# One ring over all PSUM banks, score slots in threes, and the last slot behind the value products (squared-ReLU attention into a SwiGLU block)

## The chip, the cores and the metric

The kernel runs on one core of one Trainium2 chip. A time is the device time of one execution in microseconds, from start to end; several executions give a median. One execution was also recorded by the hardware profiler. Its span runs from the first to the last recorded instruction, so its own time is a little longer than its span.

## The reference: what is computed

Inputs are q, k and v with 8 batch elements, 12 heads, 448 positions and 64 features per head, and three weight matrices (768 x 1536 twice, 1536 x 768) with a gain vector of 768. Cut to what matters:

```python
scores = np.matmul(q, k.transpose(0, 1, 3, 2)) / np.sqrt(64)
attn   = np.maximum(scores, 0.0) ** 2 / 448
x      = np.matmul(attn, v).transpose(0, 2, 1, 3).reshape(8 * 448, 12 * 64)
xn     = x / np.sqrt(np.mean(x * x, axis=-1, keepdims=True) + 1e-6) * rms_g
g      = xn @ w_gate
out    = (g * sigmoid(g) * (xn @ w_val)) @ w_out          # 3584 x 768, float32
```

There is no softmax, so no sum over keys has to be known before the value products start.

## The kernel before

**Units.** Attention is cut into 24 units `m`: batch element `b = m // 3`, and within it `t = m % 3`, four heads (two pairs). Within a unit the scores are computed transposed, keys on partitions and the 448 queries along the row, in seven *slots*. Slots 0 to 2 are the three chunks of 128 keys for the first pair of heads, slots 3 to 5 those for the second pair, and slot 6 holds the last 64 keys of both pairs.

**A slot.** `scores` (line 317) issues a slot's matmuls (line 334). In slots 0 to 5 there are two, one for each head of the pair, and each uses 64 of the 128 rows of TensorE's array; in slot 6 there are four, and each uses one 64 x 64 quadrant. They write a tile of two PSUM banks (`psS`). ScalarE then takes the relu of both banks into an SBUF tile `r` (line 343), and VectorE squares `r` in place (line 310).

**The value products.** `attend(m)` (line 437) multiplies the seven squared slots of a unit with v, into two accumulators `psAV` of one bank each: twelve matmuls of 128 rows by 64 columns for slots 0 to 5, and then four in 64 x 64 quadrants for slot 6. `evacuate` (lines 462 and 464) reads each accumulator on ScalarE, once scaled into `xT`, and from batch element 2 on once more squared into `sq`; VectorE adds up the squares (line 474).

**The dense block.** When the three units of a batch element are done, `norm` (lines 523, 531, 542, 545) makes the normalised rows `xn`. The dense work then stands in a list, `pieces`: 12 *gate* pieces (six matmuls of 448 columns into `psG`, line 614, then Silu on ScalarE, line 622), alternating with 12 *val* pieces (six matmuls into `psV`, line 628, then on VectorE the product of `psV` and the gate's `sig` into `hT`, line 635). After each second batch element come 14 *output* pieces (twelve matmuls of 384 columns into `psO`, line 657; the copy to SBUF alternates between ScalarE, line 673, and VectorE, line 675). The first batch element's dense work is done in smaller pieces (`part_gates`, line 569).

**The order.** Every engine works through its own instructions in the order in which the program issues them; nothing reorders them. The main loop at line 803 interleaves attention and dense work by hand: `fill(us)` issues pieces from the list until their estimated cost has used up `us`. For one unit of the steady part the loop issues: slots 0 and 1 of unit `m`; `attend(m - 1)`; slots 2 and 3; a fill of 0.36 of the unit's `rate`; slots 4 and 5; a fill of 0.36; slot 6; a fill of 0.28. `rate` is 4.0 for the first units, then 12.0, then 13.4. After the last unit the rest of the list is issued.

**PSUM.** PSUM has eight banks. Four of them are two `psS` tiles of two banks, used in turn. The other four are the `rot` tiles of one bank each, used in turn by everything else: gate, val and output pieces, the accumulators, the norm's sum, transposes. The framework in which the kernel is written adds the waits: an instruction that writes into a tile waits, by a semaphore, until those that used the tile before have finished.

The functions that the change touches, with the line numbers that the profile uses:

Of the kernel before, what the change touches and what calls it, by code (L numbers as in the profile page):

```python
# [15 lines left out]
def kernel(  # L16
# [37 lines left out]
    def cols(h):  # L54
# [11 lines left out]
        tc.tile_pool(name="psum", bufs=2, space=bass.MemoryType.PSUM)  # L66
# [12 lines left out]
    nc.vector.memset(ones_bf[:], 1.0)  # L79

# [114 lines left out]
    def transposes(n):  # L195
# [4 lines left out]
        if n < HP:  # L200
            pass
        elif pr == 0 or pr == 1 and e == 0:
            r0, r1 = (HALF, P) if pr == 0 else (0, P)
            if j == 0 and pr == 1:
                big(pr, None)
            ps = psum.tile([P, NU, r1 - r0], BF16, name="psQ", tag="rot", bufs=4)
            for u in range(NU):
                turn(ps[:, u, :], lambda hh: q_t[pr][:, 2 * j + hh, u, :], r0, r1)
            nc.vector.tensor_copy(out=QT[pr][:, j, :, r0:r1], in_=ps[:])
        if b == 1:  # L210
            if j == 0:
                big(None, b)
            ps = psum.tile([P, XT0], BF16, name="psK", tag="rot", bufs=4)
# [7 lines left out]
            nc.vector.tensor_copy(out=KTt[b][:, j, :XT0], in_=ps[:])  # L221
# [18 lines left out]
    def first_q(h, t, pairs=(0, 1)):  # L240
# [3 lines left out]
        ps = psum.tile([P, n, u1 - u0, HALF], BF16, name="psQ", tag="rot", bufs=4)  # L244
# [9 lines left out]
        nc.vector.tensor_copy(out=QT[0][:, j : j + n, u0:u1, :HALF], in_=ps[:])  # L254

    def first_k(t, pairs=(0, 1)):

        w, n, i0 = (S if t else XT0), len(pairs), pairs[0]
        ps = psum.tile([P, n, w], BF16, name="psK", tag="rot", bufs=4)
# [16 lines left out]
        nc.vector.tensor_copy(out=KTt[0][:, j : j + n, :w], in_=ps[:])  # L276
# [9 lines left out]
    def last_keys(m):  # L286

        b, t = divmod(m, ND)
        ps = psum.tile([P, 2, XK], BF16, name="psX", tag="rot", bufs=4)
        for i in range(2):  # L290
            turn(ps[:, i, :], lambda hh: kx_t[b][:, 4 * t + 2 * i + hh, :], 0, XK)
        nc.vector.tensor_copy(out=KTt[b][:, 2 * t : 2 * t + 2, XT0:S], in_=ps[:])
# [4 lines left out]
    def warm_tile():  # L297
        W["ps"] = psum.tile([P, S], FP32, name="psW", tag="rot", bufs=4)

    def warm(k):  # L300
        for _ in range(k):
            nc.tensor.matmul(  # L302
                out=W["ps"][:], lhsT=ones_bf[:, :P], rhs=ones_bf[:], start=True, stop=True
            )
# [12 lines left out]
    def scores(m, slots, k=0, late=None):  # L317
        b, t = divmod(m, ND)
        qt, kt = QT[b // 2], KTt[b]
        for s in slots:  # L320
            warm(k)
            ps = psum.tile([P, 2, 512], FP32, name="psS", tag="psS")
            if s < 2 * NCH:
                i, c = divmod(s, NCH)
                todo = [(2 * t + i, slice(0, P), slice(c * P, (c + 1) * P))]
            else:
                todo = [
                    (2 * t + i, slice(i * XK, (i + 1) * XK), slice(XT0, S))
                    for i in range(2)
                ]  # L330
            for j, rows, keys in todo:
                for hh in range(2):
                    prt = slice(hh * D, (hh + 1) * D)
                    nc.tensor.matmul(  # L334
                        out=ps[rows, hh, :S].rearrange("k (u x) -> k u x", u=NU),
                        lhsT=kt[prt, j, keys],
                        rhs=qt[prt, j, :, b % 2 * HALF : (b % 2 + 1) * HALF],
                        start=True,
                        stop=True,
                    )  # L340
            r = rpool.tile([P, 1024], BF16, name="r", tag="r")
            r = r[:, : 2 * S].rearrange("p (h x) -> p h x", h=2)
            nc.scalar.activation(out=r, in_=ps[:, :, :S], func=ACT.Relu)  # L343
            square(r, late)
            R[m, s] = r
# [4 lines left out]
    def part_scores(h, t, tiles, k=0, late=None):  # L350
# [4 lines left out]
        for x in tiles:  # L355
            warm(k)
            n = len(PARTS[x])
            ps = psum.tile([P, 2, 512], FP32, name="psS", tag="psS")
# [28 lines left out]
    def part_attend(h, t, late=None):  # L387
        w = (US[h][1] - US[h][0]) * HALF
        acc = [psum.tile([P, w], FP32, name="psAV", tag="rot", bufs=4) for _ in range(2)]
# [24 lines left out]
        accs = [(slice(i, i + 1), acc[i][:]) for i in range(2)]  # L414
        evacuate(0, t, accs, cols(h), late)

    def attend(m):
        b, t = divmod(m, ND)
        acc = [psum.tile([P, S], FP32, name="psAV", tag="rot", bufs=4) for _ in range(2)]
# [24 lines left out]
        evacuate(b, t, [(slice(i, i + 1), acc[i][:]) for i in range(2)], slice(0, S))  # L444
# [68 lines left out]
    def norm(b, parts, ready):  # L513
# [6 lines left out]
        ps = psum.tile([P, S], FP32, name="psSS", tag="rot", bufs=4)  # L520
# [39 lines left out]
    def part_gates(h, fbs):  # L560
# [4 lines left out]
        def both(w_sb, fb, name):  # L565
            ps = psum.tile([P, 2, w], FP32, name=name, tag="rot", bufs=4)
# [13 lines left out]
        def gate(fb, st):  # L580
# [3 lines left out]
            ps = both(wg_sb, fb, "psG")  # L584
            sig = tpool.tile([P, 512], BF16, name="sig", tag="sig")
            st["sig"] = sig[:, : 2 * w].rearrange("p (i x) -> p i x", i=2)
            nc.scalar.activation(out=st["sig"], in_=ps[:], func=ACT.Silu)

        def val(fb, st):
            ps = both(wv_sb, fb, "psV")  # L590
# [14 lines left out]
    def gates(b):  # L605
# [3 lines left out]
        def gate(fb, st):  # L609
            if e == 0:  # L610
                HT[pr, fb] = hpool.tile([P, NU, P], BF16, name="hT", tag="hT")
            ps = psum.tile([P, S], FP32, name="psG", tag="rot", bufs=4)
            for kt in range(KT):
                nc.tensor.matmul(  # L614
                    out=ps[:],
# [6 lines left out]
            nc.scalar.activation(out=sig[:, :S], in_=ps[:], func=ACT.Silu)  # L622
            st["sig"] = sig

        def val(fb, st):
            ps = psum.tile([P, S], FP32, name="psV", tag="rot", bufs=4)
            for kt in range(KT):
                nc.tensor.matmul(  # L628
                    out=ps[:],
# [8 lines left out]
                in1=ps[:].rearrange("p (u x) -> p u x", u=NU),  # L638
# [11 lines left out]
    def outproj(pr):  # L650
        ob = out[2 * pr * S : 2 * (pr + 1) * S, :].rearrange("(x u) m -> x u m", u=NU)

        def half(u, o):
            ost = opool.tile([P, OW], FP32, name="ost", tag="ost")
            ps = psum.tile([P, OW], FP32, name="psO", tag="rot", bufs=4)
            for fk in range(FT):
                nc.tensor.matmul(  # L657
                    out=ps[:],
# [13 lines left out]
            if o == 0:  # L672
                nc.scalar.copy(out=ost[:], in_=ps[:])  # L673
            else:
                nc.vector.tensor_copy(out=ost[:], in_=ps[:])  # L675
# [127 lines left out]
    for m in range(ND, N + 1):  # L803
        rate = 4.0 if m < 2 * ND + 1 else 12.0 if m < 4 * ND else 13.4
        quick = 2 if m in (2 * ND, 2 * ND + 1) else 1
        if m > ND:
# [57 lines left out]
```

## Time and profile before

| | before |
|---|---|
| median of 3 runs | 466.06 us (463.85 to 468.08) |
| the profiled execution's own time | 462.43 us |
| its span, first to last instruction | 460.7 us |
| mean granted TensorE clock | 0.999 |
| TensorE matmuls busy | 447.8 us (97% of the span), 3250 instructions |
| ScalarE busy | 271.0 us (59%) |
| VectorE busy | 259.2 us (56%) |
| GpSimd busy | 67.1 us (15%) |

A row of the timeline gives a start in microseconds from the start of the span, a duration, the engine (PE is TensorE's matmuls, PEld its weight loads, ACT is ScalarE, DVE is VectorE), the source line, the operation, output and inputs with their shapes, and how many equal instructions were merged into the row. In brackets stands how long the engine idled before the row and what released it. The end of a matmul is modelled: successive groups overlap by their pipeline's length, so the distance between two starts is the better measure of a group's cost.

### The profile page before, as it was taken

The numbers are of one execution on the slowest core, as the hardware profiler recorded it, in microseconds if no ns is written. First come the engines' busy times: TensorE is split into PE (matmuls) and PEld (weight loads), VectorE is DVE, ScalarE is ACT, GpSimd is POOL, SyncE is SP. The second block draws the span as 40 slices with busy tenths as digits, with TensorE's granted clock in tenths as the row PEclk, the third lists the DMA queues.
The fourth block names the chain that finished last, engine by engine and source line by source line (L and its number), as shares of the span: only waits on it lengthen the run. The fifth ranks groups of instructions, "written<-read, shape, count | busy, mean of one in ns | idle before, by whom it ended". The sixth has DMA issues, their size and how long they took to land.

```text
span 460.7 us, 8008 instructions
## 1 busy us (share of the span) xinstructions
PE 447.8 (97%) x3250; PEld 234.1 (51%) x3250; DVE 259.2 (56%) x466; ACT 271.0 (59%) x414; POOL 67.1 (15%) x72
## 2 busy tenths in 40 slices
PE   7898899999999999999999999999999999999997
PEld 3466565744455544444445544444445555555564
DVE  3576877966467446955576446845476436423111
ACT  3697779767656678655766568665765645222111
POOL 9534312430220017000400010000000000000000
PEclk9999999999999999999999999999999999999999
DMA  9999999999396659900896547000001210000122
GB/s 100 190 194 193 187 171 141 191 164 139 19 175 157 150 121 148 117 18 2 79 129 116 142 113 68 1 2 0 2 34 70 77 61 0 1 0 2 47 98 96
DMA packets 134181, 42.79 MB, mean 93 GB/s; under 512 B 114560, under 2 KB 134144, under 8 KB 134144
## 3 DMA queue, kind: packets, MB, share of 16 engines
q0 software_dynamic: 97056, 24.38, 63.5%
q1 hardware_dynamic: 36944, 17.80, 16.8%
q8 instruction: 25, 0.41, 0.4%
q10 hardware_dynamic: 144, 0.10, 0.1%
q14 instruction: 12, 0.10, 0.1%
HBM read 48.76 MB, written 11.01 MB: 130 GB/s over the span
## 4 chain that ended last, share of the span: by engine, by line
PE 83%; DVE 5%; DMA 4%; ACT 3%; issue 2%; POOL 1%; SPq 1%; ACTq 0%; POOLq 0%
PE psO L657 24%; PE psV L628 20%; PE psG L614 20%; PE psS L334 7%; PE psAV L437 6%; DMA KT<-kld 3%; DMA kld<-in_k_dram 1%; DVE xn L545 1%; ACT r L343 1%; DVE r L310 1%; PE psV L569 1%; PE psG L569 1%; PE psW L302 1%; PE psSS L523 1%; ACT r L382 1%
## 5 line engine op out<-in xcount | busy, mean ns | idle before, releaser
L310 DVE TENSOR_TENSOR r<-r 128x896 bf16<-128x896 bf16 (+4 forms) x171 | 103.2, 614 | 79.9 <-ACT r L343 76.5
L343 ACT ACTIVATE r<-psS 128x896 bf16<-128x896 f32 x147 | 128.6, 930 | 22.4 <-PE psS L334 22.3
L657 PE MATMUL psO<-wo_sb,hT 128*128 128x384 bf16 x672 | 113.2, 327 | 0.7 <-DVE hT L635 0.7
L614 PE MATMUL psG<-xn,wg_sb 128*128 128x448 bf16 x504 | 109.4, 353 | 0.2 <-DVE xn L545 0.2
L628 PE MATMUL psV<-xn,wv_sb 128*128 128x448 bf16 x504 | 109.3, 353 | 0.1
L622 ACT ACTIVATE sig<-psG 128x448 bf16<-128x448 f32 x84 | 46.1, 553 | 79.1 <-PE psG L614 72.9
L657 PEld LDWEIGHTS <-hT 128*128 128x128 bf16 x672 | 64.1, 98 | 47.3 <-issue 5.1
L635 DVE TENSOR_TENSOR hT<-sig,psV 128x448 bf16<-128x448 bf16 x84 | 51.3, 616 | 53.4 <-PE psV L628 51.1
L628 PEld LDWEIGHTS <-wv_sb 128*128 128x128 bf16 x504 | 47.9, 98 | 48.1 <-issue 4.8
L614 PEld LDWEIGHTS <-wg_sb 128*128 128x128 bf16 x504 | 48.0, 98 | 47.2 <-issue 4.0
L673 ACT COPY ost<-psO 128x384 f32<-128x384 f32 x28 | 13.5, 481 | 60.4 <-PE psO L657 46.9
L334 PE MATMUL psS<-QT,KT 64*128 64x448 bf16 (+1 forms) x336 | 44.5, 360 | 1.4 <-DMA KT<-kld 0.8
L675 DVE COPY ost<-psO 128x384 f32<-128x384 f32 x27 | 15.0, 554 | 29.7 <-PE psO L657 28.9
L545 DVE SCALAR_TENSOR_TENSOR xn<-xT,g_sb,rstd 128x448 bf16<-128x448 bf16 (+2 forms) x54 | 31.3, 626 | 0.2
L121 POOL DMA_DIRECT2D vld<-in_v_dram x9 | 8.9, 986 | 152.3 <-PE psAV L437 151.1
L437 PE MATMUL psAV<-r,vld 128*64 128x448 bf16 x252 | 27.8, 357 | 0.0
L542 DVE RECIPROCAL rstd<-rstd 128x112 f32<-128x112 f32 (+2 forms) x32 | 25.2, 823 | 3.5 <-ACT rstd L531 3.5
L334 PEld LDWEIGHTS <-KT 64*128 64x128 bf16 (+1 forms) x336 | 11.6, 96 | 28.0 <-issue 25.6
L382 ACT ACTIVATE r<-psS 128x768 bf16<-128x768 f32 (+3 forms) x24 | 18.5, 830 | 10.0 <-PE psS L371 10.0
L462 ACT ACTIVATE xT<-psAV 128x448 bf16<-128x448 f32 x36 | 19.8, 551 | 4.5 <-PE psAV L437 4.4
L464 ACT ACTIVATE sq<-psAV 128x448 f32<-128x448 f32 x36 | 20.0, 556 | 0.0
L437 PEld LDWEIGHTS <-vld 128*64 128x64 bf16 x252 | 12.5, 109 | 13.8 <-issue 7.4
(59 smaller groups left out, 287.6 us busy)
## 6 DMA issues: line engine op xcount, KB each, us to landing
out_dram<-ost SPq DMA_DIRECT2D x55, 192.0 KB, 2.0
qld<-in_q_dram POOLq DMA_DIRECT2D x7, 672.0 KB, 18.6
kld<-in_k_dram POOLq DMA_DIRECT2D x7, 576.0 KB, 16.0
vld<-in_v_dram POOLq DMA_DIRECT2D x7, 576.0 KB, 7.3
wo_sb<-in_moe_w_out_dram POOLq DMA_DIRECT2D x3, 768.0 KB, 28.0
vxld<-in_v_dram POOLq DMA_DIRECT2D x16, 96.0 KB, 7.3
wg_sb<-in_moe_w_gate_dram POOLq DMA_DIRECT2D x4, 384.0 KB, 14.5
wv_sb<-in_moe_w_val_dram POOLq DMA_DIRECT2D x4, 384.0 KB, 15.4
```

What stands on the lines that cost most here:

```text
L310: nc.vector.tensor_tensor(out=r, in0=r, in1=r, op=ALU.mult)
L334: nc.tensor.matmul(out=ps[rows, hh, :S].rearrange("k (u x) -> k u x", u=NU), lhsT=kt[prt, j, keys], rhs=qt[prt, j, :, b % 2 * HALF : (b % ...
L343: nc.scalar.activation(out=r, in_=ps[:, :, :S], func=ACT.Relu)
L382: nc.scalar.activation(out=r, in_=ps[:, :, : n * w], func=ACT.Relu)
L437: nc.tensor.matmul(out=acc[i][hh * D : (hh + 1) * D, :], lhsT=w[rows, hh, :], rhs=r[rows, hh, :], start=(c == 0), stop=(c == NCH),)
L542: nc.vector.reciprocal(out=rstd[:, cs], in_=rstd[:, cs])
L545: nc.vector.scalar_tensor_tensor(out=xn[:, kt, sl], in0=xt[:, kt, sl], scalar=g_sb[:, kt : kt + 1], in1=rstd[:, :w], op0=ALU.mult, op1=ALU ...
L614: nc.tensor.matmul(out=ps[:], lhsT=wg_sb[:, kt, fb * P : (fb + 1) * P], rhs=xn[:, kt, :], start=(kt == 0), stop=(kt == KT - 1),)
L622: nc.scalar.activation(out=sig[:, :S], in_=ps[:], func=ACT.Silu)
L628: nc.tensor.matmul(out=ps[:], lhsT=wv_sb[:, kt, fb * P : (fb + 1) * P], rhs=xn[:, kt, :], start=(kt == 0), stop=(kt == KT - 1),)
L635: nc.vector.tensor_tensor(out=HT[pr, fb][:, :, e * HALF : (e + 1) * HALF], in0=st["sig"][:, :S].rearrange("p (u x) -> p u x", u=NU), in1=p ...
L657: nc.tensor.matmul(out=ps[:], lhsT=HT[pr, fk][:, u, :], rhs=wo_sb[:, fk, o * OW : (o + 1) * OW], start=(fk == 0), stop=(fk == FT - 1),)
```

## The change: what it does

The two kinds of PSUM tile give way to four tiles `pb0` to `pb3` of two banks each, allocated once. `bank()` hands out one bank (half of such a tile), and `both_banks()` hands out a whole tile. Up to the fourth unit the old division is kept: tiles `pb0` and `pb1` for score slots, the four halves of `pb2` and `pb3` in turn for the rest. From the fifth unit on (`m = 4`) all eight banks are one ring in the order pb0 first half, pb0 second half, pb1 first half, and so on. Each request takes the next bank; a request for both banks first steps over a single half, so that it starts on a whole tile. The two accumulators of `attend` are now the halves of one tile.

The unit is issued in another order. Slots 0, 1 and 2 come together. Then comes `attend(m - 1)`, and directly behind its last matmuls, which work in quadrants, slot 6 of unit `m`. Before the evacuation of the accumulators is issued, the relu of slot 2 is; the relu and the square of slot 6 come behind that evacuation. Then a fill of 0.36, a fill of 0.18, slots 3, 4 and 5 together, and a fill of 0.46.

```diff
     psum = ctx.enter_context(
-        tc.tile_pool(name="psum", bufs=2, space=bass.MemoryType.PSUM)
+        tc.tile_pool(name="psum", bufs=1, space=bass.MemoryType.PSUM)
     )
...
+    banks = [
+        psum.tile([P, 2, 512], FP32, name=f"pb{i}", tag=f"pb{i}") for i in range(4)
+    ]
+    at = {"ring": None, "slot": 0, "rot": 0}
+
+    def bank(n=512, dtype=FP32):
+        if at["ring"] is None:
+            i = 4 + at["rot"] % 4
+            at["rot"] += 1
+        else:
+            i = at["ring"] % 8
+            at["ring"] += 1
+        ap = banks[i // 2][:, i % 2, :]
+        if dtype is BF16:
+            ap = ap.bitcast(BF16)
+        return ap[:, :n]
+
+    def both_banks():
+        if at["ring"] is None:
+            i = at["slot"] % 2
+            at["slot"] += 1
+        else:
+            at["ring"] += at["ring"] % 2
+            i = at["ring"] // 2 % 4
+            at["ring"] += 2
+        return banks[i]
...
-    def scores(m, slots, k=0, late=None):
+    def products(m, s):
...
-            ps = psum.tile([P, 2, 512], FP32, name="psS", tag="psS")
+        ps = both_banks()
...
+    def relu2(m, s, ps, late=None):
+        r = rpool.tile([P, 1024], BF16, name="r", tag="r")
+        r = r[:, : 2 * S].rearrange("p (h x) -> p h x", h=2)
+        nc.scalar.activation(out=r, in_=ps[:, :, :S], func=ACT.Relu)
+        square(r, late)
+        R[m, s] = r
+
+    def scores(m, slots, late=None):
         for s in slots:
...
+            relu2(m, s, products(m, s), late)
...
-    def attend(m):
+    def attend(m, after=None):
         b, t = divmod(m, ND)
-        acc = [psum.tile([P, S], FP32, name="psAV", tag="rot", bufs=4) for _ in range(2)]
+        pair = both_banks()
+        acc = [pair[:, i, :S] for i in range(2)]
...
-        evacuate(b, t, [(slice(i, i + 1), acc[i][:]) for i in range(2)], slice(0, S))
+        if after is not None:
+            after()
+        evacuate(b, t, [(slice(i, i + 1), acc[i]) for i in range(2)], slice(0, S))
...
         def gate(fb, st):
...
-            ps = psum.tile([P, S], FP32, name="psG", tag="rot", bufs=4)
+            ps = bank(S)
...
         def val(fb, st):
-            ps = psum.tile([P, S], FP32, name="psV", tag="rot", bufs=4)
+            ps = bank(S)
...
         def half(u, o):
             ost = opool.tile([P, OW], FP32, name="ost", tag="ost")
-            ps = psum.tile([P, OW], FP32, name="psO", tag="rot", bufs=4)
+            ps = bank(OW)
...
     for m in range(ND, N + 1):
...
+        if m == ND:
...
+            at["ring"] = 2 * (at["slot"] % 2)
+            continue
+        if m % ND == 0:
+            turn_by_dma(len(turns))
+        if m < N:
+            scores(m, (0, 1))
+            third = products(m, 2)
             if m == 2 * ND + 1:
                 fill(0.36 * rate, quick)
+
+            def rest(m=m, third=third):
+                relu2(m, 2, third)
+                last = products(m, 2 * NCH)
+                late.append(lambda: relu2(m, 2 * NCH, last))
+
+            attend(m - 1, rest)
+            flush(late)
+        else:
             attend(m - 1)
-            if m < N:
-                scores(m, (2, 3))
-            fill(0.36 * rate, quick)
+        fill(0.36 * rate, quick)
         if m < N - 1:
             transposes(2 * m + 2)
...
-        if m > ND and m % ND == 0:
+        if m % ND == 0:
             b = m // ND - 1
             norm(b, slice(0, S), lambda b=b: gates(b))
+        fill(0.18 * rate, quick)
         if m < N:
-            scores(m, (4, 5))
-        fill(0.36 * rate, quick)
-        if m < N:
-            scores(m, (6,))
+            scores(m, (3, 4, 5))
         if m + 1 < N:
             transposes(2 * m + 3)
-        fill(0.28 * rate, quick)
+        fill(0.46 * rate, quick)
```

Every other request for a `rot` tile (transposes, the norm's sum, the partial scores and accumulators of the first batch element) becomes a `bank()` or `both_banks()` in the same way. No arithmetic is added or removed.

## Prediction

> **What bounds it now.** I read the page's busy times first, then the chain that ended last, then the timeline of the stages.
>
> ```profile
> PE 447.8 (97%) x3250; PEld 234.1 (51%) x3250; DVE 259.2 (56%) x466; ACT 271.0 (59%) x414; POOL 67.1 (15%) x72
> ...
> PE 83%; DVE 5%; DMA 4%; ACT 3%; issue 2%; POOL 1%; SPq 1%; ACTq 0%; POOLq 0%
> ```
>
> TensorE is busy 97% of the span and makes 83% of the chain. In the list of waits none of its matmuls waits longer than 1.4 us. So whatever makes TensorE wait now lengthens the kernel, and a saving on TensorE shortens it. ScalarE and VectorE have 40% of their time free, but only as long as TensorE runs ahead of them.
>
> The stretch without attention shows how:
>
> ```profile
> 427.56 1.30 PE L614 MATMUL psG<-xn,wg_sb 128*128 128x448 bf16 x6
> ...
> 428.69 1.30 PE L628 MATMUL psV<-xn,wv_sb 128*128 128x448 bf16 x6
> 428.89 0.54 ACT L622 ACTIVATE sig<-psG 128x448 bf16<-128x448 f32 x1 [1.73 <-PE psG L614]
> ...
> 430.10 0.62 DVE L635 TENSOR_TENSOR hT<-sig,psV 128x448 bf16<-128x448 bf16 x1 [1.65 <-PE psV L628]
> ```
>
> A gate begins at 427.56 and the val piece 1.135 us later (piece to piece in this stretch), while Silu still has to read the gate's bank: it runs 428.89 to 429.43. The next piece never waits for the reader of the one before.
>
> **The saving: fewer changes of array shape.** Whenever TensorE goes from dense pieces (128 x 128) to slots (64 x 128), value products (128 x 64) or quadrants (64 x 64), time is lost. Take slot 6:
>
> ```profile
> 197.98 1.30 PE L614 MATMUL psG<-xn,wg_sb 128*128 128x448 bf16 x6
> ...
> 199.20 0.38 PE L334 MATMUL psS<-QT,KT 64*64 64x448 bf16 x4
> ...
> 199.52 1.31 PE L628 MATMUL psV<-xn,wv_sb 128*128 128x448 bf16 x6
> ```
>
> Without it the val piece would start at 197.98 + 1.135 = 199.115; it starts at 199.52. Four quadrants side by side need one pass of 448 columns (1.135/6 = 0.19), so two changes cost 0.405 - 0.19 = 0.215. Slots 4 and 5 at 194.07 give 0.21 in the same way, and the stretch from 203.03 to 205.57 (five changes) 0.58: about 0.11 a change. A unit has nine changes before and six after, over 20 units 60 x 0.11 = **-6.8 us**.
>
> **The cost: halves of one tile wait for each other.** The diff doesn't show this; the order of the built program with its semaphores does. Before, no matmul waits for a reader of another bank. After, the unit of waiting is the two-bank tile: a group that writes the second half waits for the reader of the first half, which is the group issued just before it. The val piece in pb3's second half waits for the Silu that reads pb3's first half. Following each wait value to the instruction that raises its counter, I count 114 such groups from the ring's start on (50 of them gates behind vals, 23 vals behind gates or the norm), and 12 earlier. Behind the waiting matmul all of TensorE stands still.
>
> *A bare wait.* Gate then val: from the rows above, Silu ends 1.87 us after the gate's start, against 1.135: with the restart, 0.80 late. Val then gate: the product ends at 430.72, 2.03 after the val's start: 0.95 late. Output pieces start 1.95 apart; a copy starts 2.15 after its piece (429.83 and 431.98) and takes 0.48 on ScalarE, 0.55 on VectorE: 0.74 and 0.82. The restart takes 0.06, by the one place where an output piece waited for `hT`, which ended at 235.34:
>
> ```profile
> 234.72 0.62 DVE L635 TENSOR_TENSOR hT<-sig,psV 128x448 bf16<-128x448 bf16 x1 [0.70 <-ACT sig L622]
> ...
> 235.40 0.34 PE L657 MATMUL psO<-wo_sb,hT 128*128 128x384 bf16 x1 [0.74 <-DVE hT L635]
> ```
>
> *The first wait behind a value product* is longer, because the reader stands at the end of ScalarE's queue: relu of slots 0, 1, 2, four evacuations, relu of slot 6, and only then a Silu; on VectorE the square of slot 6 stands ahead of the product.
>
> ```profile
> 188.95 0.56 ACT L462 ACTIVATE xT<-psAV 128x448 bf16<-128x448 f32 x1
> ...
> 189.38 0.58 ACT L464 ACTIVATE sq<-psAV 128x448 f32<-128x448 f32 x1
> ...
> 189.80 0.59 ACT L462 ACTIVATE xT<-psAV 128x448 bf16<-128x448 f32 x1
> ...
> 190.22 0.60 ACT L464 ACTIVATE sq<-psAV 128x448 f32<-128x448 f32 x1
> ...
> 203.03 0.55 PE L334 MATMUL psS<-QT,KT 64*128 64x448 bf16 x4
> 203.44 1.73 ACT L343 ACTIVATE r<-psS 128x896 bf16<-128x896 f32 x2 [0.89 <-PE psS L334]
> ...
> 204.77 0.38 PE L437 MATMUL psAV<-r,vxld 64*64 64x448 bf16 x4
> ...
> 205.08 0.55 PE L334 MATMUL psS<-QT,KT 64*128 64x448 bf16 x4
> ```
>
> Evacuations start 0.425 apart, relus 0.81 (two take 1.73), and the first relu starts 0.41 after slot 0. With slot 0 at time 0: relus at 0.41, 1.22, 2.03; evacuations at 2.85, 3.27, 3.70, 4.12; relu of slot 6 at 4.55, over at 5.47; Silu over at 5.90; square from 5.51, product over at 6.66. TensorE needs 0.67 for three slots, 1.26 for the twelve products, 0.19 for their quadrants, 0.32 for slot 6 with its change, 1.24 for the first piece: it is ready at 3.68. So val-gate waits 3.0 (3.2 where a Silu stands before slot 0), gate-val 2.3, and output pieces, ready at 4.5, wait 2.2 (VectorE copy) or 1.4. Units 7 to 23: eight val-gates, 25.2; three gate-vals, one of them 1.6, 6.2; six output pieces 12.4: **43.8 us**.
>
> *The first wait behind slots 3 to 5*, by the same steps: relus over at 2.95, square and product at 4.14; TensorE ready at 2.0: val-gate 2.2 (2.4 behind a Silu), gate-val 1.45, output pieces 1.35 and 0.74. Of 18: seven val-gates or transposes 16.4, five gate-vals 7.25, six outputs 5.05: **28.7 us**.
>
> *The other 70* from unit 7 on are bare: 43 for `hT` (40.9), 13 for Silu (10.4), 9 output pairs (7.3), 5 around the norm, where ScalarE loads its table (1.28) and takes the square root (0.63) first, 2.2 each (11), and 1.8 for tables loaded back: **71.4 us**. A third of these lie behind the last unit.
>
> *Units 4 to 6:* nine waits, priced alike, with transposes among them whose copy queues behind three squares (2.9 each): **17.9 us**. *The 12 earlier:* no row prices all of them; TensorE waited 0.40 for a `QT` copy once before, and some lie beside waits for loads, so between 0 and 10 us; I take **7 us**.
>
> What hides nothing here: DMA queues keep their order and data; loads and output stores have slack (output stores land in 2.0 us), and the value products' own waits (squares, v) are older than before.
>
> Sum: 43.8 + 28.7 + 71.4 + 17.9 + 7 - 6.8 = **+162 us**, on the profiled execution's 462.4: 624. The median shown, 466.06, is 3.6 above that execution; I forecast **626 us**.
>
> [...] In the rows above, the val piece writes its bank (428.69 on) while Silu reads the gate's (428.89 on), undisturbed. [...] The granted clock is 0.999 throughout. [...]
>
> **Rivals.** *Bare waits only:* if ScalarE and VectorE have caught up more than my walk says, all 126 waits cost their bare 0.90 on average (58.6 us over the 65 above that aren't around the norm): 113 - 6.8 = +106, 569 us. For it: the engines gain idle time as TensorE waits. Against: their queue order is fixed. 0.10.
>
> *The clock drops:* my longest gaps are near 3 us, one a unit. At the start, the ten warm-up matmuls of 448 columns (line 302) take 3.85 us, 0.385 each, against 0.19 warm: a cold stretch that loses 1.9 us. If each of 17 gaps brings one, +33: 659 us. Against: the clock stayed up over the small gaps of the first 40 us (TensorE is busy 79% and 94% of the first two stretches of 20 us). 0.10.
>
> *The waits don't bind, on the other side:* if the ring serves as eight independent banks, each wait points eight groups back, and only the shape changes count: 462.4 - 6.8 = 456 us, **faster**. It decides by whether the reader is the group directly before (0.80 or more late) or older than 1.1 us. The wait values say the former. 0.03; 0.01 for no change.
>
> **Range and chances.** My forecast has 0.76. Its unknowns are the long waits (72 us, perhaps a third off either way), units 4 to 6 and the start (25, half off). The range 565 to 670 takes in the bare case and the clock. Chances: faster by over 1%, 0.03; within 1%, 0.01; slower by over 1%, 0.96. About 1% is what a measurement of this kernel can tell from no change.
>
> **What would show it.** In the changed profile: TensorE busy falls to about 75%; its waits are led by the val's product on VectorE (some 50), the Silu and the output copies; behind the last unit, gate and val pieces alternate at 1.135 and 2.09 us; one gap of about 3 us follows each value product; ScalarE's and VectorE's busy times stay at 271 and 259 us. It would be wrong if those gaps are absent, if gaps are far longer than 3 us, or if matmuls of 448 columns take over 0.19 us in the middle.

## The result: 678 us, slower by 46%

| | before | changed |
|---|---|---|
| median of 4 runs each | 465.25 us (463.85 to 468.08) | 678.40 us (676.32 to 681.55) |
| the profiled execution's own time | 462.43 us | 681.55 us |
| its span | 460.7 us | 679.8 us |
| mean granted TensorE clock | 0.999 | 0.907 |

The ratio is 1.4645 (95% interval 1.458 to 1.471). The prediction was 626 us with a range of 565 to 670: the direction and most of the amount were right, and the time lies above the range. Some executions run some per cent slower at a lower granted clock (the kernel before took 481.75 us at 0.982 in one, 462.28 at 0.996 in another); the ratios leave them out, the medians and ranges do not.

The page of the changed kernel, its busy times, the granted clock in 40 slices, and the three costliest groups of matmuls (busy time, mean ns of one, idle time of TensorE ahead of them and what ended most of it):

```profile
PE 507.2 (75%) x3250; PEld 253.1 (37%) x3250; DVE 266.3 (39%) x466; ACT 271.3 (40%) x414; POOL 67.1 (10%) x72
...
PEclk7788788899989987688988988969887999999999
...
L653 PE MATMUL pb<-xn,wg_sb 128*128 128x448 bf16 x504 | 122.6, 384 | 70.0 <-DVE hT L674 63.9
L667 PE MATMUL pb<-xn,wv_sb 128*128 128x448 bf16 x504 | 123.8, 387 | 31.2 <-ACT sig L661 26.4
...
L696 PE MATMUL pb<-wo_sb,hT 128*128 128x384 bf16 x672 | 119.9, 334 | 28.5 <-DVE ost L714 16.6
```

Two things are to be seen. TensorE, which idled 12.9 us before (460.7 - 447.8), now idles 172.6 us (679.8 - 507.2): +159.7. And the same 3250 matmuls are busy 507.2 us instead of 447.8: +59.4. A gate or val matmul took 353 ns on average before and 384 or 387 now, and the granted clock, 0.999 before, is below 0.9 in 21 of the first 30 slices.

The list of waits of the changed kernel (engine, line, what released it: us in total, times, longest) leads with the three that the prediction named:

```profile
PE pb L653 <- DVE hT L674: 63.9, 50, 3.1
PE pb L667 <- ACT sig L661: 26.4, 23, 2.8
PE pb L696 <- DVE ost L714: 16.6, 13, 2.2
```

The timeline of one unit shows both effects in a row:

```profile
163.38 1.31 PE L667 MATMUL pb<-xn,wv_sb 128*128 128x448 bf16 x6
...
165.54 1.00 ACT L375 ACTIVATE r<-pb 128x896 bf16<-128x896 f32 x1
...
166.58 0.62 DVE L340 TENSOR_TENSOR r<-r 128x896 bf16<-128x896 bf16 x1 [0.18 <-ACT r L375]
167.12 0.61 DVE L674 TENSOR_TENSOR hT<-sig,pb 128x448 bf16<-128x448 bf16 x1
167.79 1.85 PE L653 MATMUL pb<-xn,wg_sb 128*128 128x448 bf16 x6 [3.11 <-DVE hT L674]
...
169.44 2.45 PE L667 MATMUL pb<-xn,wv_sb 128*128 128x448 bf16 x6
...
172.67 1.29 PE L653 MATMUL pb<-xn,wg_sb 128*128 128x448 bf16 x6 [0.78 <-DVE hT L674]
```

The val piece at 163.38 is the first one behind a value product. The gate at 167.79 writes the other half of the same tile, so it waits for the val's reader, the product at 167.12, which stands behind the relu and square of slot 6: TensorE idles 3.11 us. Then the second effect: the gate's matmuls slow down, with a granted clock of 0.50 from 168.4 to 171.7, and the val at 169.44 takes 2.45 us for six matmuls, nearly twice the 1.31 of the val at 163.38. The next gate at 172.67 is at full pace again and shows a bare wait of 0.78.

Where the time came from, stretch by stretch. The boundaries are the starts of value products; "busy" and "idle" are TensorE's. "Filled" is a later experiment in which the waits are there but the clock is full from unit 7 on; its column is its stretch less that of before.

| stretch | before | changed | difference | busy | idle | predicted | filled |
|---|---|---|---|---|---|---|---|
| start to `attend(3)` | 55.54 | 78.89 | +23.4 | +11.5 | +11.9 | +7 | +21.1 |
| `attend(3)` to `attend(6)` | 33.79 | 55.86 | +22.1 | +4.5 | +17.6 | +16.9 | +23.5 |
| `attend(6)` to `attend(23)` | 286.52 | 432.32 | +145.8 | +38.6 | +107.2 | +114.3 | +114.3 |
| from `attend(23)` on | 84.85 | 112.73 | +27.9 | +4.8 | +23.1 | +23.8 | +27.9 |
| sum | 460.7 | 679.8 | +219.1 | +59.4 | +159.7 | +162 | +186.8 |

(Predicted, from the prediction's terms: 7; 17.9 less 3 units of 0.34; 43.8 + 28.7 + two thirds of 71.4, less 17 units of 0.34; a third of 71.4.) The row that carries the miss is the third, 31.5 us over the forecast, and then the first.

### The profile page after: what moved, and what is told of

Read it like the earlier page. It is cut to its first block, busy times and chain, and to the rows that moved or that the text cites. A ratio compares the mean times of both kernels' runs of the same rounds, so it can differ in the third digit from the quotient of the medians.

```text
span 679.8 us, 8029 instructions
## 1 busy us (share of the span) xinstructions
PE 507.2 (75%) x3250; PEld 253.1 (37%) x3250; DVE 266.3 (39%) x466; ACT 271.3 (40%) x414; POOL 67.1 (10%) x72
## 3 DMA queue, kind: packets, MB, share of 16 engines
q1 hardware_dynamic: 36944, 17.80, 10.8%
## 5 line engine op out<-in xcount | busy, mean ns | idle before, releaser
L653 PE MATMUL pb<-xn,wg_sb 128*128 128x448 bf16 x504 | 122.6, 384 | 70.0 <-DVE hT L674 63.9
L667 PE MATMUL pb<-xn,wv_sb 128*128 128x448 bf16 x504 | 123.8, 387 | 31.2 <-ACT sig L661 26.4
L375 ACT ACTIVATE r<-pb 128x896 bf16<-128x896 f32 x147 | 127.6, 932 | 39.9 <-PE pb L363 39.0
L696 PE MATMUL pb<-wo_sb,hT 128*128 128x384 bf16 x672 | 119.9, 334 | 28.5 <-DVE ost L714 16.6
L661 ACT ACTIVATE sig<-pb 128x448 bf16<-128x448 f32 x84 | 46.0, 547 | 211.4 <-PE pb L653 208.6
L674 DVE TENSOR_TENSOR hT<-sig,pb 128x448 bf16<-128x448 bf16 x84 | 52.1, 620 | 190.0 <-PE pb L667 190.0
L363 PE MATMUL pb<-QT,KT 64*128 64x448 bf16 (+1 forms) x336 | 40.9, 364 | 0.2 <-DVE KT L250 0.2
L474 PE MATMUL pb<-r,vld 128*64 128x448 bf16 x252 | 27.8, 355 | 0.5 <-DVE hT L631 0.2
L418 ACT ACTIVATE r<-pb 128x768 bf16<-128x768 f32 (+3 forms) x24 | 18.5, 826 | 17.6 <-PE pb L407 17.6
L608 PE MATMUL pb<-xn,wv_sb 128*128 128x192 bf16 (+1 forms) x144 | 17.9, 281 | 8.8 <-DVE QT L238 5.8
L501 ACT ACTIVATE xT<-pb 128x448 bf16<-128x448 f32 x36 | 21.0, 585 | 3.3 <-PE pb L474 3.3
L503 ACT ACTIVATE sq<-pb 128x448 f32<-128x448 f32 x36 | 21.5, 597 | 0.0
## 6 DMA issues: line engine op xcount, KB each, us to landing
wo_sb<-in_moe_w_out_dram POOLq DMA_DIRECT2D x3, 768.0 KB, 23.1
```

The source lines that it names most:

```text
L363: nc.tensor.matmul(out=ps[rows, hh, :S].rearrange("k (u x) -> k u x", u=NU), lhsT=kt[prt, j, keys], rhs=qt[prt, j, :, b % 2 * HALF : (b % ...
L474: nc.tensor.matmul(out=acc[i][hh * D : (hh + 1) * D, :], lhsT=w[rows, hh, :], rhs=r[rows, hh, :], start=(c == 0), stop=(c == NCH),)
L608: nc.tensor.matmul(out=ps[:, i, :], lhsT=w_sb[:, kt, (fb + i) * P : (fb + i + 1) * P], rhs=XN[0][:, kt, sl], start=(kt == 0), stop=(kt == ...
L653: nc.tensor.matmul(out=ps, lhsT=wg_sb[:, kt, fb * P : (fb + 1) * P], rhs=xn[:, kt, :], start=(kt == 0), stop=(kt == KT - 1),)
L661: nc.scalar.activation(out=sig[:, :S], in_=ps, func=ACT.Silu)
L667: nc.tensor.matmul(out=ps, lhsT=wv_sb[:, kt, fb * P : (fb + 1) * P], rhs=xn[:, kt, :], start=(kt == 0), stop=(kt == KT - 1),)
```

## The experiments

My theory after the result: the waits between halves of one tile cost what the prediction says, and the rest, about 50 us, is TensorE's clock, which falls after gaps of 2 to 3 us. Rivals: the new order or the ring by itself costs much of the time; the clock does not matter by itself.

### One request, one tile

```diff
         else:
             i = at["ring"] % 8
-            at["ring"] += 1
+            at["ring"] += 2
```

From the ring's start each request for a bank takes the first half of a whole tile, so no group shares a tile with the one before. Up to the fourth unit all is as in the changed kernel. In unit 7 the bank of slot 2 is written over by the value products before its relu; that slot takes other values there, the work is the same.

> The changed kernel, but from the fifth unit on each request takes a whole two-bank tile in turn (a single request uses its first half), so no group waits for the reader of the group just before it. The first four units keep their halves. Theory 1 (halves wait for each other, and the gaps bring the clock down): the first value products still come some 23 us late, and from there on the saved shape changes are all that is left: 465 + 23 - 7 = 481 us, between 470 and 492, granted clock near 1 behind the first 90 us. Rival (the new order of slots itself holds TensorE up behind ScalarE's queue): the two-bank waits explain only some 100 us, so 560 us or more, with gaps of about 3 us behind every value product still there.

Measured: 487.39 us (486.53 to 492.32), ratio 1.050 (1.042 to 1.059). `attend(3)` is 18.6 us late, `attend(6)` 22.8, `attend(23)` 24.1. So from the ring's start on next to nothing is left of the change's cost, and what is left was there before the ring: the start, where requests still take the halves of `pb2` and `pb3` in turn. In the 74.10 us up to `attend(3)` TensorE's busy time is 6.4 us above that of before and its idle time 12.2.

### Eight tiles of one bank

```diff
-        psum.tile([P, 2, 512], FP32, name=f"pb{i}", tag=f"pb{i}") for i in range(4)
+        psum.tile([P, 512], FP32, name=f"pb{i}", tag=f"pb{i}") for i in range(8)
...
-        ap = banks[i // 2][:, i % 2, :]
+        ap = banks[i][:]
...
-        return banks[i]
+        return banks[2 * i : 2 * i + 2]
...
-        nc.scalar.activation(out=r, in_=ps[:, :, :S], func=ACT.Relu)
+        for hh in range(2):
+            nc.scalar.activation(out=r[:, hh], in_=ps[hh][:, :S], func=ACT.Relu)
```

Ring and order are the change's own, at the start too, but the unit of waiting is the bank. A slot's relu becomes two instructions.

> The changed kernel with eight tiles of one bank in place of four of two, in the same ring and the same order; the relu of a slot becomes two instructions, one for each bank. Theory 1: no half waits for another, so the time is that of before less the shape changes, 465 - 7 = 458 us, between 452 and 464, clock 0.99 or more. Rival (order at fault): 560 us or more. If the doubled relus tell on ScalarE, 465 to 475 us.

Measured: 469.18 us (465.66 to 478.73), ratio 1.010 (1.007 to 1.014), clock 1.0. With the same banks in the same order all but 1% of the slowdown is gone, so the tile as unit of waiting makes it, not the ring. The time is above the 452 to 464 that I expected and in the band given for the doubled relus, but they are hardly what lengthens it: "One request, one tile" has single relus and loses the same 4.2 us in units 4 to 6, and about as much in the units with a norm. The start now costs 2.5 us instead of 23.4. The gain that I had put at 0.34 us a unit is there in most plain units (0.2 to 0.6 from `attend(6)` on), but it is given back: +4.2 in units 4 to 6, and +0.2 to +1.0 in four of the units with a norm (12, 15, 18, 21). The timeline of unit 12 shows how:

```profile
181.11 1.30 PE L671 MATMUL pb<-xn,wv_sb 128*128 128x448 bf16 x6
...
181.73 1.28 ACT L574 ACT_TABLE_LOAD   x1
182.25 1.30 PE L657 MATMUL pb<-xn,wg_sb 128*128 128x448 bf16 x6
...
183.68 1.28 ACT L665 ACT_TABLE_LOAD   x1
...
184.98 0.55 ACT L665 ACTIVATE sig<-pb 128x448 bf16<-128x448 f32 x1
...
185.57 1.30 PE L671 MATMUL pb<-xn,wv_sb 128*128 128x448 bf16 x6 [1.35 <-ACT sig L665]
```

The norm loads one table on ScalarE and the next Silu loads the other back, 2.56 us together; the Silu ends at 185.53. The val piece behind three score slots takes the bank again that this Silu reads, the ring having stepped over one bank, and waits 1.35.

### The long gaps filled

```diff
             i = at["ring"] % 8
             at["ring"] += 1
+            if i % 2 and at["gap"]:
+                spare = banks[(i // 2 + 1) % 4]
+                k, at["gap"] = at["gap"], 0
+                for _ in range(k if n == S else k // 2):
+                    nc.tensor.matmul(out=spare[:, 0, :S], lhsT=ones_bf[:, :P],
+                                     rhs=ones_bf[:], start=True, stop=True)
...
             attend(m - 1, rest)
             flush(late)
+            at["gap"] = 13 if m > 2 * ND else 0
...
             scores(m, (3, 4, 5))
+            at["gap"] = 6 if m > 2 * ND else 0
```

The changed kernel, and from unit 7 on matmuls that compute nothing stand in the gap behind the value products (13) and behind slots 3 to 5 (6).

> The changed kernel with dummy matmuls of 448 columns (13, or 6 before an output piece) in the first gap behind each value product, and 6 (3) in the first gap behind slots 3 to 5, from unit 7 on; they write a bank that is free, and every wait stays. Theory 1 with the clock: the gaps stay as long but are filled, the granted clock behind the first 135 us rises from about 0.92 to 0.97 or more, and the time falls by 20 to 35 us, to 645 to 660 us. Rival (the clock costs nothing, all of the loss is in the waits): 678 us or up to 15 us more, as the dummies that end late delay the next piece.

Measured: 656.19 us (653.49, 658.88), ratio 1.411 (1.396 to 1.426); clock 0.958 (0.99 from 135 us on, where the changed kernel has 0.93). The same place as above, in this kernel's timeline:

```profile
162.74 1.31 PE L678 MATMUL pb<-xn,wv_sb 128*128 128x448 bf16 x6
163.88 2.62 PE L99 MATMUL pb<-ones_bf 128*128 128x448 bf16 x13
167.15 1.29 PE L664 MATMUL pb<-xn,wg_sb 128*128 128x448 bf16 x6 [0.65 <-DVE hT L685]
168.28 1.30 PE L678 MATMUL pb<-xn,wv_sb 128*128 128x448 bf16 x6
```

From the first val piece to the gate it is 4.41 us, as in the changed kernel (163.38 to 167.79): the wait is not shortened. But the gate is followed by the next val after 1.13 us instead of 1.65, and that val is at full pace. Doing useless work on TensorE made the kernel 22 us shorter. That is the clock, and it is about what the theory says for units 7 on.

### Only the halves

```diff
-            ps = psum.tile([P, S], FP32, name="psG", tag="rot", bufs=4)
+            ps = bank(S)
...
-        acc = [psum.tile([P, S], FP32, name="psAV", tag="rot", bufs=4) for _ in range(2)]
+        pair = both_banks()
+        acc = [pair[:, i, :S] for i in range(2)]
```

and so for every request for a `rot` tile, while `at["ring"]` stays `None`: the kernel before with its own order, two tiles for score slots, and its four rotating banks made halves of two tiles. One more thing differs, which the expectation leaves out: `attend` gets its two accumulators from `both_banks()`, so they take one of the two tiles of the score slots instead of two rotating banks.

> The kernel of before in its old unit order and with its old division of PSUM into two score tiles and four rotating banks; only that the four rotating banks are now the halves of two persistent two-bank tiles. Theory 1: 101 groups behind the fourth unit and 12 earlier wait for the reader of the group just before them, 90 us bare, some 35 more behind value products and slots, 30 to 40 for the clock: 610 to 660 us. Rival (the halves cost little, the loss is the ring's or the order's): 465 to 500 us.

Measured: 650.25 us (648.44, 652.06), ratio 1.398 (1.384 to 1.412); clock 0.960. A kernel in the order of before, with nothing added, takes 40% longer. Its waits are led by

```profile
PE pb L667 <- ACT sig L661: 40.1, 58, 2.5
PE pb L363 <- ACT sq L503: 28.2, 17, 1.7
PE pb L474 <- ACT r L375: 17.4, 19, 1.0
PE pb L653 <- DVE hT L674: 15.0, 12, 2.7
```

The second and third row, 45.6 us, come from the accumulators: score slots wait for the evacuation of a tile that is now theirs too, and value products for a slot's relu. The other two are waits between halves, mostly for the Silu, since gates happen to take first halves. TensorE idles 161.1 us (646.7 - 485.6), 148.2 more than before; less the 45.6, about 103 are left for the halves and all else. So this run shows that halves cost much without the new order, but its 1.40 is not their price alone, and that it falls into the expected range of 610 to 660 is partly luck.

### Only the order

The loop of the changed kernel on the tiles of before (`psS` twice, `rot` four times); nothing shares a tile.

```diff
-            at["ring"] = 2 * (at["slot"] % 2)
...
-        ps = both_banks()
+        ps = psum.tile([P, 2, 512], FP32, name="psS", tag="psS")
...
-        pair = both_banks()
-        acc = [pair[:, i, :S] for i in range(2)]
+        acc = [psum.tile([P, S], FP32, name="psAV", tag="rot", bufs=4) for _ in range(2)]
```

> The new unit order alone: PSUM divided as before (two score tiles, four rotating banks, each a tile of its own). Slot 2 now needs the tile of slot 0, and slot 5 that of slot 3, so TensorE waits for a relu (0.41 + 0.92 behind the slot's start, against 0.48 that two slots take: some 0.85 us) twice a unit, 20 units: 34 us; less 7 for the shape changes: 490 us, between 478 and 505, granted clock 0.99. If the order itself were what costs 200 us in the changed kernel: over 560 us.

Measured: 511.30 us (510.63, 511.97), ratio 1.101 (1.093 to 1.108): 21 us more than I expected. Its list of waits is led by one line:

```profile
PE psS L333 <- ACT r L345: 40.7, 41, 2.3
```

Three slots in a row need three tiles, and there are two: the third slot waits about 1 us for the relu of the first, twice a unit. From `attend(7)` on a plain unit costs 1.7 us more than before. So the order by itself is a loss; it needs the ring's extra tiles, which is the part of the change that works. About 10 us more came in units 5 and 6, where TensorE waited 3.1 us for a load of k and the granted clock was 0.85 (the twelve matmuls of a value product behind that wait took 2.45 us, elsewhere 1.32); I take no conclusion from those.

### The order late, on four whole tiles

As before through unit 7; from unit 8 on the change's order, with all eight banks as four tiles of two banks, one per request. In the first version the norm stands one piece earlier.

```diff
+    ring["pool"] = ctx.enter_context(
+        tc.tile_pool(name="ring", bufs=4, space=bass.MemoryType.PSUM)
+    )
+    for m in range(2 * ND + 2, N + 1):
...
+            attend(m - 1, rest)
+            flush(late)
+        fill(0.27 * rate)
...
+            norm(b, slice(0, S), lambda b=b: gates(b))
+        fill(0.27 * rate)
+        if m < N:
+            scores(m, (3, 4, 5))
...
+        fill(0.46 * rate)
```

> A version meant to keep what the change gains: everything as before through unit 7; from unit 8 on the new order on a ring of four two-bank tiles, each request a tile of its own, relu in one instruction; and the norm's sum one piece earlier, so that its table loads end before slots 3 to 5. With eight separate banks the plain units ran 0.2 to 0.5 us faster than before, the units with a norm 0.2 to 1.0 slower, units 4 to 6 together 4.2 slower, the start 2.5 slower. Theory 1: 12 plain units at -0.35 and 4 with a norm at about 0: 465 - 4 = 461 us, ratio to before 0.985 to 0.995. Rival: the change of pools or the norm's units cost as much as is gained: ratio 0.998 to 1.005.

Measured: 463.02 us (460.78 to 468.73, 12 runs), ratio 0.997 (0.992 to 1.001). In the profile the distance from `attend(7)` to `attend(23)` is 2.5 us shorter than before, plain units 0.1 to 0.56 each, the norm units (9, 12, 15, 18, 21) +0.31, +0.07, -0.52, +0.67, -0.19. The second version has the norm where the change puts it (fills of 0.36 and 0.18):

> As the version that keeps everything through unit 7 as before, but with the norm's sum where the change puts it, a piece later. Theory 1: the four units with a norm lose about 1 us each again (the Silu before slots 3 to 5 waits for two table loads of 1.28 and a square root), so 3 to 4 us slower than with the sum a piece earlier. Rival: where the sum stands doesn't matter, within 1 us.

Measured: 469.38 us (463.30 to 478.88, 13 runs) against 467.71 of the same comparison, ratio 1.004 (0.999 to 1.008). Neither interval excludes no change, the two overlap, and the runs of that comparison spread widely. The profiles tell the versions apart: from `attend(7)` to `attend(23)` the second takes 3.5 us longer than the first, within the 3 to 4 expected, and in units 12, 15 and 21, where the val piece now waits for the Silu, 1.1 to 1.3 us each. The gain of the new order without the added waits is thus at most 0.8%, under the 5.4 us (1.2%) that 16 units of 0.34 would give, and I can't tell it from nothing in the times.

### All gaps filled

```diff
+            if i % 2 and at["last"] == i - 1:
+                spare = banks[(i // 2 + 1) % 4]
+                k, at["gap"] = at["gap"] or 4, 0
+                for _ in range(k if n == S else max(3, k // 2)):
+                    nc.tensor.matmul(...)
+            at["last"] = i
```

> The changed kernel with matmuls of 448 columns that compute nothing, into a bank of the next tile, in every gap between the two halves of a tile from the ring's start on: 13 (6 up to unit 6) behind value products, 6 behind slots 3 to 5, 4 elsewhere, half as many before output pieces. The waits stay, since the second half's group still waits for the reader of the first. Theory (waits, and on top of them a clock that falls in the long gaps): mean granted clock 0.97 or more, the matmuls of 448 columns in the middle back to 0.35 mean or less, time 628 to 650. Rival (the clock costs nothing by itself, the filler of the first such run only let ScalarE and VectorE catch up): no lower than that run's 656, and the fillers of the short gaps add to it.

Measured: 648.78 us (648.32, 649.24), ratio 1.395 (1.374 to 1.416); clock 0.966, just under what I expected, because the fillers begin with the ring and the start has a lowered clock here too (0.80, in the changed kernel 0.76). Windows between the same value products as in the table, of the changed kernel (stretch, its length, busy time and number of matmuls, granted clock; the last two columns, of DMA, are not used):

```profile
0.00:78.89 78.89, 59.46 (x613) 0.76 1.46 176
78.89:134.75 55.86, 37.49 (x372) 0.91 1.57 97
134.75:567.07 432.32, 324.02 (x1810) 0.91 0.37 48
567.07:679.80 112.73, 86.24 (x462) 1.00 0.07 25
```

and of this kernel:

```profile
0.00:76.66 76.66, 57.65 (x612) 0.80 1.53 168
76.66:133.99 57.33, 45.95 (x402) 0.87 1.57 113
133.99:534.76 400.77, 368.47 (x2225) 1.00 0.41 52
534.76:647.50 112.74, 107.47 (x575) 1.00 0.07 25
```

The third row is the measurement I wanted. With every wait in place and the clock at 1.00, units 7 to 23 take 400.77 us, 114.3 above before; with the clock at 0.91 they take 432.32. So the waits of these units cost about 114 and the clock about 31.5. In 40 of the 74 filled gaps of this row the next piece starts less than 0.06 us behind the fillers, so some of these may have ended after the wait: 114 is rather an upper bound. In the last row, where only short gaps stand, that is so in 22 of 30, the clock is 1.00 in both kernels, and the fillers change nothing.

### One gap of a chosen length

The kernel before, and in each unit from 8 to 23 one gap made by hand. By one theory gaps of 2 to 3 us are enough for the clock to fall, by the other only longer ones are.

```diff
+    def idle(k):
+        warm_tile()
+        warm(1)
+        for _ in range(k):
+            nc.scalar.copy(out=W["ps"][:], in_=W["ps"][:])
+        warm(1)
...
-        fill(0.28 * rate, quick)
+        if 2 * ND + 1 < m < N:
+            fill(0.14 * rate, quick)
+            idle(1)
+            fill(0.14 * rate, quick)
```

> The kernel before with one gap made by hand in each unit from 8 to 23 (16 of them): one matmul of 448 columns into a spare bank, one ScalarE copy of that bank onto itself, one matmul more. TensorE stands still for the copy and what ScalarE has queued ahead of it, 0.9 to 1.5 us. Both theories: 16 gaps and 32 matmuls of 0.19, +20 to +30 us on the kernel before, and the clock stays at 0.99 or more.

> The same with four copies: gaps of 2.3 to 3.0 us. Theory (the clock falls after gaps of 2 to 3 us): 10 or more of the 16 gaps are followed by a stretch at a lower clock that loses some 2.5 us, mean granted clock 0.93 to 0.97, and the time is 25 to 40 us above what the gaps and the matmuls themselves take (+45 to +55), so +70 to +95 on the kernel before. [...]

> The same with six copies: gaps of 3.3 to 4.0 us. Both theories: nearly all 16 gaps bring a stretch at a lower clock, clock 0.92 to 0.96, +62 to +72 for gaps and matmuls and 35 to 45 for the clock, so +97 to +117 on the kernel before.

Measured: 483.68 us (482.49, 484.87) with one copy, 531.40 (525.37, 537.43) with four, 563.97 (556.50, 571.44) with six, against 464.64. In the profiled executions of the last two the stretch from `attend(3)` to `attend(6)`, ahead of the first gap, is also 17 us longer than before, with waits for loads of k and q (4.3 and 4.8 us with four copies) and a lowered clock behind them (there 0.66 from 70 to 100 us), so I compare from `attend(7)` to `attend(23)`. The other execution of each, 60.7 and 91.9 us above before, agrees with the stretches below.

| copies | gap, mean (range) | gaps followed by a slow stretch | `attend(7)` to `attend(23)`, over before |
|---|---|---|---|
| 1 | 0.75 (0.60 to 0.88) | 0 of 16 | +20.4 |
| 4 | 2.4 (2.25 to 2.52) | 7 of 16 | +57.8 |
| 6 | 3.5 (3.35 to 3.62) | 14 of 16 | +89.9 |

(A slow stretch: a microsecond with a granted clock under 0.8 within the next five.) With four copies the nine units without a slow stretch cost 2.94 us each on average, that is the gap, the two matmuls and the changes around them; 16 of those are 47.0, and the other 10.8 us make 1.5 for each of the seven slow stretches. With six copies 16 x (3.49 + 0.54) = 64.5, which leaves 25.4, 1.8 for each of 14. So gaps of 2.25 to 2.52 us do not leave the clock alone; but I had expected 10 or more of 16, and 2.5 us each, so four copies stay under the +70 to +95 expected, and one copy, with +19.0, just under its +20 to +30. Two of the gaps of the kernel with four copies, of equal length and with the same work behind them:

```profile
198.45 0.35 PE L302 MATMUL psW<-ones_bf 128*128 128x448 bf16 x1 [2.52 <-ACT psW L310]
198.64 1.69 PE L635 MATMUL psV<-xn,wv_sb 128*128 128x448 bf16 x6
200.12 2.45 PE L621 MATMUL psG<-xn,wg_sb 128*128 128x448 bf16 x6
...
220.61 0.35 PE L302 MATMUL psW<-ones_bf 128*128 128x448 bf16 x1 [2.52 <-ACT psW L310]
220.80 1.30 PE L635 MATMUL psV<-xn,wv_sb 128*128 128x448 bf16 x6
221.93 1.30 PE L621 MATMUL psG<-xn,wg_sb 128*128 128x448 bf16 x6
```

Behind the first, the val piece slows down midway and the gate piece runs at half pace throughout; behind the second nothing happens. Here are the microseconds from the one on in which each gap ends (the first busy time is TensorE's, the third number from the end is the granted clock):

```profile
198.00:199.00 1.00, 0.55 (x3) 0.29 (x3) 0.00 (x0) 0.40 (x1) 0.00 (x0) 1.00 0.65 123
199.00:200.00 1.00, 1.00 (x5) 0.48 (x4) 0.00 (x0) 0.00 (x0) 0.00 (x0) 0.70 0.63 121
200.00:201.00 1.00, 1.00 (x4) 0.43 (x3) 0.56 (x1) 0.00 (x0) 0.00 (x0) 0.50 0.35 61
201.00:202.00 1.00, 1.00 (x5) 0.32 (x3) 0.06 (x1) 0.00 (x0) 0.00 (x0) 0.50 0.00 0
202.00:203.00 1.00, 1.00 (x6) 0.13 (x4) 0.00 (x0) 0.39 (x1) 0.00 (x0) 0.59 0.00 0
203.00:204.00 1.00, 1.00 (x13) 0.58 (x12) 0.01 (x1) 1.00 (x3) 0.00 (x0) 1.00 0.00 0
...
220.00:221.00 1.00, 0.39 (x3) 0.20 (x3) 0.88 (x2) 0.53 (x2) 0.00 (x0) 1.00 4.30 142
221.00:222.00 1.00, 1.00 (x7) 0.54 (x6) 0.00 (x0) 0.00 (x0) 0.00 (x0) 1.00 4.07 148
222.00:223.00 1.00, 1.00 (x7) 0.42 (x5) 0.80 (x2) 0.00 (x0) 0.00 (x0) 1.00 4.57 144
223.00:224.00 1.00, 1.00 (x10) 0.37 (x10) 1.00 (x2) 0.73 (x2) 0.00 (x0) 1.00 4.66 144
224.00:225.00 1.00, 1.00 (x16) 0.44 (x10) 0.36 (x2) 1.00 (x2) 0.00 (x0) 1.00 4.74 160
225.00:226.00 1.00, 1.00 (x10) 0.35 (x11) 0.81 (x2) 1.00 (x3) 0.00 (x0) 1.00 2.88 90
```

So the length of a gap gives only a chance, here 7 of 16; I leave open what else decides.

## Why the prediction was wrong where it was

**TensorE as the bound, and the halves as the cost: right.** Taking the sharing away (one request, one tile; eight tiles) takes the slowdown away from the ring's start on. Putting the sharing into the order of before brings most of the idle time back, though not all of that run's 1.40 is its doing. TensorE's busy share is 75%, as forecast, the named waits lead, and ScalarE's busy time stays at 271.3; VectorE's rose from 259.2 to 266.3, which I did not follow up (the product that the gates wait for takes 620 ns on average, 616 before).

**Sizes of the waits: right.** Behind the last unit gate and val pieces start 1.13 and 2.08 us apart in turn, where 1.135 and 2.09 were forecast:

```profile
621.34 1.29 PE L653 MATMUL pb<-xn,wg_sb 128*128 128x448 bf16 x6 [0.78 <-DVE hT L674]
...
622.47 1.30 PE L667 MATMUL pb<-xn,wv_sb 128*128 128x448 bf16 x6
...
624.55 1.29 PE L653 MATMUL pb<-xn,wg_sb 128*128 128x448 bf16 x6 [0.78 <-DVE hT L674]
```

The first wait behind a value product was priced 3.0 and is 3.11 where shown. Over units 7 to 23 the terms come to 114.3, and the kernel with all gaps filled measures 114.3; so close a sum owes something to errors that cancel. One pair is known: of the saving of 5.8 us in this sum the kernel with eight tiles shows 0.6, so the waits themselves took at most some 115 where 120 were priced. Behind the last unit 23.8 were priced and 27.9 measured.

**The clock: the step that failed.** The prediction's sum has no term for a lowered clock. That the clock would stay up behind gaps of 3 us was my assumption, which no run shows: no matmul of before waited longer than 1.4 us. The rival *The clock drops* got 0.10 at 659 us. The runs show that the clock falls behind such gaps, and that the sum lacked a term of 31.5 us for it. In the changed kernel, of the gaps from 80 us on that began at full clock, 3 of 9 of 1.8 to 2.2 us were followed by a slow stretch, 6 of 9 of 2.3 to 2.4, and 11 of 13 of 2.7 to 3.1. The rival's price was good: 17 times 1.9 is 33, and units 7 to 23 have 17 slow stretches, 13 of 3.4 us and four of 6.8 to 10.2, which cost 31.5. Its reason against, that the clock had stayed up over the small gaps of the first 40 us, concerned gaps of some tenths of a microsecond and could say nothing of gaps of three.

**The 12 earlier waits: undersized.** I gave them 0 to 10 us and took 7, with no row for most of them. The start takes 23.4 more, and 2.5 with eight tiles. Idle time alone is 11.9, over the upper bound; another 11.5 is busy time at a lowered clock (0.76 in this stretch, 1.00 before). There it fell behind gaps of 0.90 and 0.45 us. Windows of the changed kernel's start:

```profile
5.00:6.00 1.00, 0.30 (x12) 1.00 1.26 92
6.00:7.00 1.00, 0.36 (x6) 1.00 1.21 95
7.00:8.00 1.00, 0.99 (x15) 0.98 1.50 161
8.00:16.00 8.00, 6.96 (x66) 0.50 1.67 180
16.00:25.00 9.00, 7.98 (x86) 0.50 1.46 197
```

In the two microseconds from 5 on TensorE is busy 0.66 in all (1.46 before, where the clock stays at 1.00), and from 8 to 25 it has half the clock although it is then busy 87 to 89%. The low clock lasts 17.1 us (7.96 to 25.02), longer than any slow stretch of units 7 to 23. Why the start is different stays open.

**Units 4 to 6: 16.9 priced, 22.1 measured.** Idle time accounts for 17.6 of it; the rest is busy time at a clock of 0.91.

**The saving: right in kind, worth next to nothing.** Plain units without the added waits gain up to 0.6 us each, about the 0.34 that I had priced. But the norm units and units 4 to 6 give it back, which I had not priced at all. In the kernel with eight tiles, whose start adds 2.5, the sum is +6.1 us in the profile. That kernel also bears on the rival *The waits don't bind*, 456 us: even where the halves don't wait for each other, the change is not faster.

**The range** ended at 670 although the rival stood at 659 by itself and the start's term had no row: the misses of the four rows, 16.4 + 5.2 + 31.5 + 4.1 = 57.2, all have the same sign and make the 219.1 of the 162. Most of them share one cause: in the first three stretches, where added waits lie close together, the granted clock was 0.76, 0.91 and 0.91, against 1.00 before, and I had treated the terms as independent.

## What to carry to other kernels

Before two banks are put into one tile, ask who waits for what: a tile is the unit in which the added semaphores work, and two groups that are issued one behind the other must not share one, even where they touch different banks (ratio 1.4645 with two banks in a tile, 1.010 with one). When an edit makes the bounding engine stand still, price the lower clock afterwards as part of the main sum: here 11 of 13 gaps of 2.7 to 3.1 us in the changed kernel and 14 of 16 of 3.35 to 3.62 with six copies were followed by a slow stretch, and one cost 1.5 to 1.9 us. To tell a wait from its consequences, fill the gap with work that computes nothing: what remains is the wait.

## What was not expected of the hardware

The granted clock fell already after gaps shorter than 3 us: after 7 of 16 of 2.25 to 2.52 us; after gaps of 3.35 to 3.62 it fell in 14 of 16, and after gaps of 0.60 to 0.88 in none of 16. At the start of the changed kernel it also fell, to 0.50, with no gap over 0.9 us, after two microseconds (from 5 us on) in which TensorE was busy 0.66 in all. At the lowered clock, 0.50, six matmuls of 448 columns take 2.45 us instead of 1.31. A kernel with 560 more matmuls (3810 against 3250) was 30 us faster than the same kernel without them (648.78 against 678.40).
